# A spectral mixing layer and an ELU feed-forward on one core: tokens ordered by quarters, x read in strided chunks, the first batch's start rearranged

## The chip, the cores and the metric

The kernel runs on one core of a Trainium2 chip. The metric is the device time in microseconds; of several runs the median counts. Engines are named as in the profile: PE (TensorE, with PEld for its weight loads), DVE (VectorE), ACT (ScalarE), POOL (GpSimd) and SP (SyncE, here only an issuer of DMAs).

## The reference

For each of 8 batches of 3008 tokens by 256 channels: a real Fourier transform along the tokens, a complex linear layer with a soft threshold, the inverse transform; then a feed-forward with ELU over all tokens.

```python
X = np.fft.rfft(x, axis=1)
Yr = Xr @ w_r - Xi @ w_i + b_r
Yi = Xr @ w_i + Xi @ w_r + b_i
Yr = np.sign(Yr) * np.maximum(np.abs(Yr) - lam, 0.0)      # Yi likewise
y = np.fft.irfft(Yr + 1j * Yi, n=3008, axis=1)
h = y @ w_in                                              # 256 -> 2048
g = np.where(h > 0.0, h, np.exp(np.minimum(h, 0.0)) - 1.0)
out = g @ w_out                                           # 2048 -> 256
```

## The kernel before

The Fourier transform of length 3008 is split into 47 x 64, so a token has two indices; in the code a token is `r * 32 + n`, with `r` of 94 and `n`, the second index, of 32. Everything is written as matrix products with tables made on the chip from sines.

A batch goes through these units, each a few matmuls on PE into PSUM, followed by one copy out:

- **A** (8 units, L111): the first short transform. `load_x` (L93) reads x in four chunks of 8 neighbouring `n`, on POOL's queue, as two DMAs of 80 and 14 partitions; a partition gets 8 neighbouring rows, 8 KB in one piece. Two units work on a chunk; the result goes to DRAM (`DA`).
- **Z** (`load_Z`, L138): three pieces read back from `DA`, turned so that the other index lies on the partitions. A piece is four DMAs.
- **X** (6 units, L148): the second short transform, two units (`dt` 0 and 1) a piece, copied to `XT`.
- **M** (12 groups, L167 to L208): the complex linear layer, bias and soft threshold, giving `Y`. DVE adds the bias (`yb`); then POOL clips and subtracts, or, for some groups of batch 0, ACT clips and DVE finishes (`let_go`, one group later).
- **B** (6 units, L210): the first half of the inverse; to DRAM (`DB`), and read back as four tiles `Bs` (L240), one for each quarter of `n`.
- **Y** (8 units, L249): the second half. Units `2w` and `2w + 1` take the `Bs` of quarter `w` and write `yT`, the transposed input of the feed-forward. Before the change the tokens of `yT` lie in their natural order, so that each unit writes 8 of every 32 tokens.

The **feed-forward** runs over all 8 batches as one stream of steps. A batch has 48: six blocks of tokens (five of 512, one of 448), and in each eight pairs of feature tiles. `front(i)` (L521) makes `hps` with four matmuls and starts ACT's Exp (`Et`); `elu` (L539) makes `gT` with two DVE instructions; `back(i - 2)` (L547) adds to the block's output in PSUM with eight matmuls, and at a block's end ACT copies it to `osb` and SP issues its DMA, one for all whole tiles of 128 tokens and one for the rest. Since a block's tokens lie across all of `n`, its first `front` needs all eight Y units of its batch.

The order on every engine is the order in which the program is written (`tc.manual_schedule()`); an engine works its queue strictly in turn. `plan(b)` (L591) places units into the steps of batch `b`: list `f1` between `front` and `elu`, list `f2` behind `back`. In batch `b` run X, M, B and Y of batch `b + 1` and A of batch `b + 2`; batch 0 also carries A of batch 1, and the last batch carries nothing. In batches 1 to 6 the units X to A lie in steps 2 to 33, Y in steps 40 to 47. The units of the loop share one PSUM tile (`psF`, L507).

**Batch 0** goes through the units ahead of the loop ("alone"), with PSUM pools of its own (`pre2`, `pre1`, `pre0`, L72 to L74). Two things stand in the order there: DVE computes the sine arguments for the table M2 (`wrap`, L315) in three groups, ACT turns them into sines behind that group's copies of A (L363 to L382), and `idle_pe` (L266) issues matmuls whose result nobody reads, which keep PE at work while it would wait. Behind them come the load of the feed-forward's weights, X, M and B of batch 0 (L468 to L492), the reading of `Bs`, 28 idle matmuls, and eight Y units. `gate` (L452) makes POOL wait for a tile before it issues the loads behind it.

## Time and profile before

| | us |
|---|---|
| median of three runs | 1008.99 (1007.75 to 1010.56) |
| the profiled execution | 1007.92 |
| its span, first to last instruction | 1005.8 |
| first `gT` of the loop starts | 87.13 |
| batches 1 to 5, each | about 115.7 |

A profile page shows the busy time of each engine, the span in slices, the DMA queues, the chain of work that ended last, the costliest groups of instructions and the DMAs. A row of the timeline gives the start, the busy time, the engine, the line, the operation, the tiles with their shape, and in brackets the idle time before it and what ended that. A row of the windows gives the stretch, its length, each engine's busy time with its count of instructions, the clock granted to PE (1.00 is full), the share of the DMA engines and the bytes they moved.

### The profile page before, as it was taken

The numbers are of one execution on the slowest core, as the hardware profiler recorded it, in microseconds if no ns is written. First come the engines' busy times: TensorE is split into PE (matmuls) and PEld (weight loads), VectorE is DVE, ScalarE is ACT, GpSimd is POOL, SyncE is SP. The second block draws the span as 40 slices with busy tenths as digits, with TensorE's granted clock in tenths as the row PEclk, the third lists the DMA queues.
The fourth block names the chain that finished last, engine by engine and source line by source line (L and its number), as shares of the span: only waits on it lengthen the run. The fifth ranks groups of instructions, "written<-read, shape, count | busy, mean of one in ns | idle before, by whom it ended". The sixth has DMA issues, their size and how long they took to land.

```text
span 1005.8 us, 16444 instructions
## 1 busy us (share of the span) xinstructions
PE 939.9 (93%) x6469; PEld 660.6 (66%) x6469; DVE 831.7 (83%) x935; ACT 625.0 (62%) x722; POOL 249.5 (25%) x262
## 2 busy tenths in 40 slices
PE   3777899999999999999999999999999999999997
PEld 1335666676667666776667766676667766677775
DVE  8346778789888998889988898889988888888886
ACT  4235666865676657675586566675676656575554
POOL 4232155015400453005500354005410144000000
PEclk9888999999999999999999999999999999999999
DMA  9939451924292244713373053812446011400011
GB/s 192 244 90 219 119 134 44 236 64 104 73 251 53 68 107 117 186 41 83 94 197 107 21 138 84 236 40 52 116 123 159 19 43 56 113 30 33 22 42 40
DMA packets 91714, 105.41 MB, mean 105 GB/s; under 512 B 5682, under 2 KB 81460, under 8 KB 88628
## 3 DMA queue, kind: packets, MB, share of 16 engines
q1 hardware_dynamic: 84916, 76.04, 27.3%
q0 software_dynamic: 6176, 26.74, 12.8%
q10 hardware_dynamic: 544, 1.57, 0.7%
q8 instruction: 51, 0.84, 0.4%
q14 instruction: 27, 0.22, 0.1%
HBM read 54.53 MB, written 49.81 MB: 104 GB/s over the span
## 4 chain that ended last, share of the span: by engine, by line
PE 69%; DVE 13%; ACT 10%; DMA 5%; issue 2%; POOL 0%; ACTq 0%; DVEq 0%; SPq 0%; POOLq 0%
PE hps L531 28%; PE ps_o L564 24%; DVE gT L542 8%; PE mps L172 8%; ACT Et L536 6%; DVE Et L540 4%; PE aps L120 3%; PE bps L220 3%; DMA DA<-A 2%; PE xps L156 2%; PE yps L257 2%; ACT XT L109 1%; DMA Bs<-DB 1%; DMA xt<-in_x_dram 1%; ACT yT L109 1%
## 5 line engine op out<-in xcount | busy, mean ns | idle before, releaser
L536 ACT ACTIVATE Et<-hps 128x1024 f32<-128x1024 f32 (+1 forms) x384 | 388.6, 1012 | 316.7 <-PE hps L531 314.9
L542 DVE SCALAR_TENSOR_TENSOR gT<-hps,Et 128x1024 fp32r<-128x1024 f32 (+1 forms) x384 | 461.7, 1202 | 34.9 <-DVE Et L540 0.9
L564 PE MATMUL ps_o<-w_out_r,gT 128*128 128x256 f32 (+1 forms) x3072 | 473.2, 296 | 2.1 <-ACT osb L576 1.3
L564 PEld LDWEIGHTS ps_o<-w_out_r,gT 128*128 128x128 f32 (+1 forms) x3072 | 403.9, 187 | 47.4 <-issue 8.9
L531 PE MATMUL hps<-yT,w_in_s 128*128 128x512 bf16 (+1 forms) x1536 | 392.8, 377 | 21.5 <-DVE gT L542 19.4
L540 DVE TENSOR_SCALAR Et<-Et 128x1024 f32<-128x1024 f32 (+1 forms) x384 | 279.9, 729 | 79.3 <-ACT Et L536 78.2
L531 PEld LDWEIGHTS <-w_in_s 128*128 128x128 bf16 x1536 | 127.5, 97 | 138.2 <-issue 30.8
L187 POOL TENSOR_SCALAR clip<-yb 128x512 f32<-128x512 f32 x84 | 77.0, 917 | 510.1 <-DVE yb L179 509.5
L188 POOL TENSOR_TENSOR Y<-yb,clip 128x512 bf16<-128x512 f32 x84 | 108.1, 1286 | 7.0
L179 DVE TENSOR_TENSOR yb<-mps,bias_bc 128x512 f32<-128x512 f32 x96 | 66.2, 691 | 28.9 <-PE mps L172 22.0
L172 PEld LDWEIGHTS <-XT 128*128 128x128 bf16 x384 | 37.6, 99 | 53.1 <-ACT XT L109 5.8
L109 ACT CAST A<-aps 96x1024 bf16<-96x1024 f32 x63 | 62.9, 1003 | 13.1 <-PE aps L120 8.4
L120 PE MATMUL aps<-xt,M 94*96 94x512 f32 x128 | 50.8, 487 | 16.9 <-DMA xt<-in_x_dram 10.9
L172 PE MATMUL mps<-wcat_r,XT 128*128 128x512 bf16 x192 | 59.0, 387 | 5.3 <-ACT XT L109 5.0
L172 PE MATMUL mps<-wcat_s,XT 128*128 128x512 bf16 x192 | 58.2, 385 | 0.0
L109 ACT CAST yT<-yps 128x752 bf16<-128x752 f32 x60 | 47.1, 785 | 12.9 <-PE yps L257 12.9
L576 ACT COPY osb<-ps_o 128x512 f32<-128x512 f32 x96 | 50.4, 586 | 3.7 <-PE ps_o L564 3.7
L97 POOL DMA_DIRECT2D xt<-in_x_dram x64 | 44.0, 690 | 32.1 <-PE aps L120 31.8
L109 ACT CAST XT<-xps 128x1024 bf16<-128x1024 f32 x47 | 47.1, 1006 | 7.6 <-PE xps L156 7.6
L109 ACT CAST Bz<-bps 128x1024 bf16<-128x1024 f32 x47 | 47.8, 1019 | 2.3 <-PE bps L220 2.3
L120 PEld LDWEIGHTS aps<-xt,M 94*96 94x96 f32 x128 | 20.1, 176 | 33.4 <-ACT A L109 19.0
L257 PEld LDWEIGHTS <-Bs 96*128 96x128 bf16 x512 | 28.5, 100 | 16.4 <-DMA Bs<-DB 4.5
(76 smaller groups left out, 234.1 us busy)
## 6 DMA issues: line engine op xcount, KB each, us to landing
xt<-in_x_dram POOLq DMA_DIRECT2D x32, 640.0 KB, 6.1
out_dram<-osb SPq DMA_DIRECT2D x40, 512.0 KB, 3.4
Z<-DA SPq DMA_DIRECT2D x90, 128.0 KB, 3.4
Bs<-DB SPq DMA_DIRECT2D x60, 192.0 KB, 4.6
DA<-A SPq DMA_DIRECT2D x28, 384.0 KB, 4.4
DB<-Bz SPq DMA_DIRECT2D x21, 512.0 KB, 3.4
xt<-in_x_dram POOLq DMA_DIRECT2D x32, 112.0 KB, 5.7
out_dram<-osb SPq DMA_DIRECT2D x8, 384.0 KB, 2.6
```

The lines of the kernel that those rows point to most:

```text
L109: nc.scalar.copy(dst, src)
L120: nc.tensor.matmul(ps[0 : 4 * K1, j, :], lhsT=M1[:], rhs=xt[:, 4 * uu + 2 * j : 4 * uu + 2 * j + 2, :], start=True, stop=True,)
L172: nc.tensor.matmul(ps, lhsT=XT[:, dt, c, o : o + P], rhs=wm[:, dt, :], start=(m == 0 and dt == 0), stop=(m == 1 and dt == 1),)
L179: nc.vector.tensor_tensor(yb[:], ps, bias_bc[:], ALU.add)
L187: nc.gpsimd.tensor_scalar(clip[:], yb[:], LAM, -LAM, ALU.min, ALU.max)
L188: nc.gpsimd.tensor_tensor(Y_of[b, q][:, i, :], yb[:], clip[:], ALU.subtract)
L531: nc.tensor.matmul(hps[:, s, 0:nb], lhsT=w_in_s[:, dt, ft * P : ft * P + P], rhs=yT[:, dt, bs : bs + nb], start=(dt == 0), stop=(dt == 1),)
L536: nc.scalar.activation(Et[:, :, 0:nb], hps[:, :, 0:nb], AF.Exp)
L540: nc.vector.tensor_scalar(Et[:, :, 0:nb], Et[:, :, 0:nb], 1.0, -1.0, ALU.min, ALU.add)
L542: nc.vector.scalar_tensor_tensor(gT[:, :, 0:nb], hps[:, :, 0:nb], 0.0, Et[:, :, 0:nb], ALU.max, ALU.add)
L564: nc.tensor.matmul(po[q][0 : t1 - t0, i_ % 2, :], lhsT=gT[:, s, t0:t1], rhs=w_out_r[:, ft, :], start=(ft == 0 and i_ % 2 == 0), stop=(ft = ...
L576: nc.scalar.copy(osb[:, i_ : i_ + k, :], po[i_ // 2][:, 0:k, :])
```

## The change

The order of tokens in `yT` becomes (quarter `w` of `n`, `r`, place `j` in the quarter), so a unit of Y writes 752 neighbouring tokens and a block needs only the quarters it lies in. The output's DMAs put the rows back in order: one for each 128 tokens, and two where a tile lies across two quarters. Ahead of the loop stand only Y units 0 and 1 of batch 0; units 2 to 7 of every batch now run inside that batch's own steps, units 0 and 1 of the next one behind `back` in steps 46 and 47. Chunk `ci` of x holds the `n` of the form `4 m + ci`, so a partition gets 8 rows of 1 KB instead of one piece of 8 KB; A's writes follow that. In batch 0, A's tiles lie in the four buffers of `Bs`, X units 0 to 3 stand ahead of all M, units 4 and 5 between the first M groups, and `XT` has three buffers. The idle matmuls read a constant tile, have a PSUM bank for themselves, and stand at more places: 20 at the start, 5, 5 and 3 behind units of A, 16 (14 before) ahead of X. The bias copy moves from ACT to DVE. The load of batch 1's x waits for the last `Bs` instead of the first `yT`.

```diff
-        xv = x[b].rearrange("(r n) d -> r n d", n=NH)
+        xv = x[b].rearrange("(r m c) d -> c r m d", c=4, m=8)
-            nc.gpsimd.dma_start(xt[r0:r1], xv[r0:r1, ci * 8 : ci * 8 + 8, :].bitcast(F32R))
+            nc.gpsimd.dma_start(xt[r0:r1], xv[ci, r0:r1].bitcast(F32R))
...
-            A_of[b, ci] = wk2.tile([4 * K1, 8, D], BF16, name="A", tag="A")
+            if alone:
+                A_of[b, ci] = wk4.tile([4 * K1, 8, D], BF16, name="A", tag="Bs")
+            else:
+                A_of[b, ci] = wk2.tile([4 * K1, 8, D], BF16, name="A", tag="A")
...
+        dav = DA_of[b].rearrange("(m c) r d -> c r m d", c=4)
...
+            nc.sync.dma_start(dav[ci, :, 4 * uu : 4 * uu + 4, :], A[:, 4 * uu : 4 * uu + 4, :])
...
+            nc.sync.dma_start(dav[ci], A[:])
...
-                engs[h].dma_start(Z[q : q + NH], DA_of[b][:, r : r + 8, :])
+                engs[c].dma_start(Z[q : q + NH], DA_of[b][:, r : r + 8, :])
...
-            XT_of[b, g] = wk2.tile([P, 2, 2, 8 * N2], BF16, name="XT", tag="XT")
+            XT_of[b, g] = wk3.tile([P, 2, 2, 8 * N2], BF16, name="XT", tag="XT")
...
-            yT[:, dt, :].rearrange("p (r n) -> p r n", n=NH)[:, :, 8 * w : 8 * w + 8],
-            psv[:, :, 0 : 2 * N1].rearrange("p n r -> p r n"), on_dve,
+            yT[:, dt, w * WT : w * WT + WT].rearrange("p (r j) -> p r j", j=8),
+            psv[:, :, 0 : 2 * N1].rearrange("p j r -> p r j"), on_dve,
...
+    busy = constp.tile([P, 512], BF16, name="busy")
+    nc.vector.memset(busy[:], 1.0)
+    ips = pre0.tile([P, 512], F32, name="ips", tag="pre0")
...
+            nc.tensor.matmul(ips[:], lhsT=busy[:, 0:P], rhs=busy[:], start=True, stop=True)
...
+    idle_pe(20)
...
-            if g == 2:
+            if g < 2:
+                idle_pe(5)
+            else:
+                idle_pe(3)
                 unit_A(0, 6, alone=True)
                 unit_A(0, 7, alone=True, on_dve=True)
...
-        m4ps = pre0.tile([P, 512], F32, name="m4ps", tag="pre0")
+        m4ps = pre1.tile([P, 512], F32, name="m4ps", tag="mps1")
...
-        bb = pre0.tile([P, 2 * D], F32, name="bb", tag="pre0")
+        bb = pre1.tile([P, 2 * D], F32, name="bb", tag="mps1")
-        nc.scalar.copy(bias_bc[:], bb[:])
-        idle_pe(14)
+        nc.vector.tensor_copy(bias_bc[:], bb[:])
+        idle_pe(16)
...
     fX(1, True)
+    fX(2)
+    fX(3, True)
     first_M(0, 0, True)
+    fX(4)
     first_M(0, 1, False)
+    fX(5)
     first_M(1, 0, True)
     first_M(1, 1, False)
-    fX(2)
-    fX(3)
     first_M(2, 0, True)
+    fB(0)
...
-    for u in range(8):
+    for u in range(2):
         unit_Y(0, u, alone=True, on_dve=bool(u % 2))
-    gate(yT_of[0][:, 0, 0:1])
+    gate(Bs_of[0, 3][:, 0, 0:1])
...
+        ov = out[b * S : b * S + S, :].rearrange("(r w j) e -> w r j e", w=4, j=8)
+        for q in range((nsub + 1) // 2):
...
+            for i_ in range(2 * q, 2 * q + k):
+                t, end = bs + i_ * P, min(bs + i_ * P + P, bs + nb)
+                while t < end:
+                    w, r0 = t // WT, t % WT // 8
+                    t1 = min(end, (w + 1) * WT)
+                    p0, n8 = t - bs - i_ * P, (t1 - t) // 8
+                    nc.sync.dma_start(
+                        ov[w, r0 : r0 + n8], osb[p0 : p0 + 8 * n8, i_, :]
+                    )
+                    t = t1
...
         if b == 0:
+            for u in range(2, 8):
+                f1[u - 1].append(put("Y", 0, u))
             for u in range(8):
-                f1[2 + u].append(put("A", 1, u))
+                f1[7 + u].append(put("A", 1, u))
-            lead, pairs = 13, [
+            lead, seq = 18, [
...
-            lead, pairs = 2, [[u] for u in (
+            lead, seq = 0, [
+                ("y", 2), ("y", 3), ("X", 0), ("X", 1), ("M", 0, 0), ("M", 0, 1), ("X", 2),
+                ("M", 1, 0), ("M", 1, 1), ("X", 3), ("B", 0), ("y", 4), ("M", 2, 0), ("M", 2, 1),
+                ("y", 5), ("X", 4), ("B", 1), ("M", 3, 0), ("M", 3, 1), ("X", 5), ("B", 2),
+                ("y", 6), ("M", 4, 0), ("M", 4, 1), ("B", 3), ("y", 7), ("M", 5, 0), ("M", 5, 1),
+                ("A", 0), ("B", 4), ("A", 1), ("B", 5), ("A", 2), ("A", 3), ("A", 4), ("A", 5),
+                ("A", 6), ("A", 7),
...
+        if n1 < B:
+            for u in range(2):
+                f2[46 + u].append(put("Y", n1, u))
```

In the lists `("y", u)` is unit `u` of Y of the batch whose steps run, the other entries are of the next batch (A of the one after it). `WT` is 752.

More of the change, by code (lines that the diff above doesn't have):

```diff
@@ L80 @@
     LAG = 2
+    WT = 2 * N1 * 8
     x_of = {}
@@ L261, in unit_Y @@
         evac(
-            yT[:, dt, :].rearrange("p (r n) -> p r n", n=NH)[:, :, 8 * w : 8 * w + 8],
-            psv[:, :, 0 : 2 * N1].rearrange("p n r -> p r n"), on_dve,
-        )
+            yT[:, dt, w * WT : w * WT + WT].rearrange("p (r j) -> p r j", j=8),
+            psv[:, :, 0 : 2 * N1].rearrange("p j r -> p r j"), on_dve,
+        )
+    busy = constp.tile([P, 512], BF16, name="busy")
+    nc.vector.memset(busy[:], 1.0)
+    ips = pre0.tile([P, 512], F32, name="ips", tag="pre0")
     def idle_pe(n):
-        ps = pre0.tile([P, 512], F32, name="idle", tag="pre0")
         for _ in range(n):
-            nc.tensor.matmul(
-                ps[:], lhsT=M2[:, 0, 0:2, :].rearrange("p a b -> p (a b)"),
-                rhs=M2[:, 0, 0:8, :].rearrange("p a b -> p (a b)"), start=True, stop=True,
-            )
+            nc.tensor.matmul(ips[:], lhsT=busy[:, 0:P], rhs=busy[:], start=True, stop=True)
+    idle_pe(20)
     with tc.tile_pool(name="stagep", bufs=1) as stagep:
@@ L571, in back @@
         osb = late2.tile([P, 4, E], F32, name="osb", tag="osb")
-        nfull, rem = nb // P, nb % P
-        row0 = b * S + bs
-        for i_ in range(0, nfull, 2):
-            k = min(2, nfull - i_)
-            nc.scalar.copy(osb[:, i_ : i_ + k, :], po[i_ // 2][:, 0:k, :])
-        nc.sync.dma_start(
-            out[row0 : row0 + nfull * P, :].rearrange("(i p) e -> p i e", p=P),
-            osb[:, 0:nfull, :],
-        )
-        if rem:
-            nc.scalar.copy(osb[0:rem, nfull, :], po[nfull // 2][0:rem, nfull % 2, :])
-            nc.sync.dma_start(
-                out[row0 + nfull * P : row0 + nb, :], osb[0:rem, nfull, :]
-            )
+        ov = out[b * S : b * S + S, :].rearrange("(r w j) e -> w r j e", w=4, j=8)
+        for q in range((nsub + 1) // 2):
+            k = min(2, nsub - 2 * q)
+            if nb >= (2 * q + k) * P:
+                nc.scalar.copy(osb[:, 2 * q : 2 * q + k, :], po[q][:, 0:k, :])
+            else:
+                for e in range(k):
+                    rows = min(P, nb - (2 * q + e) * P)
+                    nc.scalar.copy(osb[0:rows, 2 * q + e, :], po[q][0:rows, e, :])
+            for i_ in range(2 * q, 2 * q + k):
[8 more added lines that the diff above has]
+                    t = t1
         del po_of[b, blk]
@@ L594, in plan @@
         f2 = [[] for _ in range(PER)]
-        if b + 1 >= B:
-            return f1, f2
         n1, n2 = b + 1, b + 2
-        def at(t, *us, r=f1):
-            for u in us:
-                r[t].append(put(u[0], n2 if u[0] == "A" else n1, *u[1:]))
         if b == 0:
+            for u in range(2, 8):
+                f1[u - 1].append(put("Y", 0, u))
             for u in range(8):
-                f1[2 + u].append(put("A", 1, u))
-            f1[9] += [(load_Z, (1, g)) for g in range(3)]
-            lead, pairs = 13, [
[6 rows of a table removed]
+                f1[7 + u].append(put("A", 1, u))
+            f1[14] += [(load_Z, (1, g)) for g in range(3)]
+            lead, seq = 18, [
[5 rows of a table added]
             ]
-            xs = (12, 15, 18, 21)
+            xs = (16, 19, 22, 25)
         else:
-            lead, pairs = 2, [[u] for u in (
[5 rows of a table removed]
-            )]
-            xs = (3, 7, 11, 15)
-        for t, us in enumerate(pairs, lead):
-            us = [u for u in us if n2 < B or u[0] != "A"]
-            at(t, *us[:1])
-            at(t, *us[1:], r=f2)
-            if ("A", 3 if b == 0 else 4) in pairs[t - lead]:
+            lead, seq = 0, [
[6 rows of a table added]
+            ]
+            xs = (3, 7, 11, 15)
+        for t, u in enumerate(seq, lead):
+            if u[0] == "y":
+                f1[t].append(put("Y", b, u[1]))
+            elif u[0] == "A":
+                if n2 < B:
+                    f1[t].append(put("A", n2, u[1]))
+            elif n1 < B:
+                if u[0] == "X" and len(u) == 3:
+                    f1[t].append(put("X", n1, u[1]))
+                    f2[t].append(put("X", n1, u[2]))
+                else:
+                    f1[t].append(put(u[0], n1, *u[1:]))
+            if u == ("A", 3) and n1 < B:
                 f2[t] += [(load_Bs, (n1, w)) for w in range(4)]
@@ L634, in plan @@
                 f1[xs[ci]].append((load_x, (n2, ci)))
-        for u in range(8):
-            at(40 + u, ("Y", u), r=f2 if f1[40 + u] else f1)
+        if n1 < B:
+            for u in range(2):
+                f2[46 + u].append(put("Y", n1, u))
         return f1, f2
```

16 lines of the change are left out of this document (3 added, 13 removed), and 16 rows, old and new, of tables (f2, xs).

## The prediction

> **What bounds the kernel now.** I read the page's first part, then the busy time by stage (the cuts are the moments at which one kind of work hands over to the next), then the chain of waits.
>
> ```profile
> PE 939.9 (93%) x6469; PEld 660.6 (66%) x6469; DVE 831.7 (83%) x935; ACT 625.0 (62%) x722; POOL 249.5 (25%) x262
> ```
>
> ```profile
> core 0: us, PE busy (x) PEld busy (x) DVE busy (x) ACT busy (x) POOL busy (x), PEclk, DMA share, GB/s
> 0.00:27.55 27.55, 10.01 (x34) 5.62 (x35) 22.05 (x53) 13.03 (x17) 11.58 (x22) 1.00 0.88 188
> 27.55:37.48 9.93, 6.93 (x27) 3.05 (x24) 1.38 (x2) 0.58 (x1) 0.89 (x2) 0.83 0.89 235
> 37.48:68.81 31.33, 22.44 (x149) 10.28 (x148) 15.62 (x21) 13.60 (x16) 13.64 (x14) 0.86 0.61 147
> 68.81:83.02 14.21, 10.21 (x90) 6.00 (x89) 5.43 (x8) 3.14 (x4) 4.45 (x9) 0.86 0.91 207
> 83.02:87.13 4.11, 3.73 (x8) 1.09 (x8) 1.43 (x2) 1.17 (x2) 0.00 (x0) 0.50 1.13 223
> ...
> 210.86:326.54 115.68, 113.51 (x802) 80.77 (x801) 100.39 (x108) 77.14 (x90) 31.94 (x32) 1.00 0.43 109
> ```
>
> From 87 us on TensorE is busy 98% of a batch at full clock: the loop is bound by the work put into its steps. Before 87 us five stages run one after the other. Only in the first is an engine near full (VectorE, 22 of 27.55 us); the others have the clock at 0.5 to 0.86 and are held by waits. That is where the change works. The chain of waits names the holders:
>
> ```profile
> 23.98 1.22 DVE A L107
> ...
> 25.22 2.23 DMA DA<-A
> ...
> 27.98 3.96 DMA Z<-DA
> ...
> 32.30 0.59 ACT bias_bc L423
> ...
> 32.94 4.70 PE idle L270 x14
> ...
> 68.83 2.79 DMA DB<-Bz
> ...
> 73.01 8.28 DMA Bs<-DB
> ```
>
> All sums below are against this profiled execution (span 1005.8, 1007.92 with what lies around it); the median of the runs, 1008.99, lies 1.07 above it.
>
> **Stage 1, x and A (0 to 27.55).** Two things change: x comes in 1 KB pieces instead of 8 KB, and A gets four buffers.
>
> ```profile
> 1.39 2.30 POOL L97 DMA_DIRECT2D xt<-in_x_dram  x4 [0.18 <-issue]
> ...
> 20.41 0.69 DVE L318 TENSOR_TENSOR v<-r,v 128x512 f32<-128x512 f32 x1
> 20.74 1.92 ACT L109 CAST A<-aps 96x1024 bf16<-96x1024 f32 x2 [3.55 <-DMA DA<-A]
> ```
>
> ```profile
> L450 POOL DMA_DIRECT2D w_out_r<-in_moe_w_out_dram x2 | 1.9, 952 | 0.3 <-issue 0.3
> ```
>
> ```profile
> 41.00:46.00 5.00, 3.16 (x27) 1.81 (x25) 3.75 (x5) 1.53 (x3) 3.76 (x4) 1.00 1.84 354
> ```
>
> Speed of the load: w_out, in 1 KB pieces, flows at 354 GB/s (41 to 46 us); x of batch 1, in 8 KB pieces, at 223 (83 to 87 us). So small pieces cost nothing here, and x is likely to land earlier. That gains nothing by itself, since ScalarE's copies of A stand behind the sines, and these behind VectorE's sine arguments. Issue: a w_out DMA of 1,024 pieces held POOL for 952 ns; four x DMAs of 80 and 14 pieces held it 2.30 us, 575 each. Their new counts are 640 and 112, so by a line between the two rows (0.4 ns a piece) the four take 2.8 us (+0.5); all at 952 would be +1.5. kv is queued behind them on POOL, and VectorE's long run of sine arguments behind kv: +0.5 on that run, which ended at 21.10 and will end at 21.6. The wait of 3.55 us (ScalarE for an A buffer) goes; what is late next is that VectorE run, behind which the last A's copy stands: 1.22 + 2.23 for its DMA, so Z can be issued at about 25.2 instead of 27.55: **-2.35** (bounds +1, if all of kv's and more delay comes, to -3).
>
> The 33 new idle matmuls lie in TensorE's 17 free microseconds of this stage; even at half clock the first 20 end (20 x 0.43) by the time A can start. Their memset runs while VectorE still waits for POOL's first iota. Z's four DMAs a piece are split between SP and ScalarE's queue by c instead of h, two on each as before: nothing.
>
> **Stage 2, Z to the first X (27.55 to 37.48).** Z's first piece has landed by 31.94, yet X starts at 37.48 (the cut): ScalarE issues Z's DMAs, then the bias copy (32.30), and the 14 idle matmuls wait for that bank, 4.70 us. After: the copy is on VectorE and the idle matmuls have a bank of their own, so they follow `bb`.
>
> ```profile
> 25.57 0.15 PEld L404 LDWEIGHTS m4ps<-ident,M1p 94*96 94x96 f32 x1 [2.46 <-issue]
> ...
> 28.45 1.49 PE L422 MATMUL bb<-brow,ones 1*128 1x512 f32 x2
> ```
>
> `bb` ends 4.37 us after the M4 transpose, which follows the last A's copy by 0.37 (25.20 to 25.57): now 22.85 + 0.37 + 4.37 = 27.6. Sixteen matmuls then take 3.45 us at full clock (0.215 each, rows of stage 3) or 5.1 with eight at half clock: X at 31.05 to 32.7. Z lands at 25.2 + 4.4 = 29.6, before that. I take 32.0, in between: the stage is 6.8 instead of 9.93, **-3.1** (bounds -2 to -5). M3's third bank now waits for M4's copy and `bb` for M3's first copy; both copies are done while the transposes run.
>
> The row of 14 idle matmuls in 4.70 us is a start at half clock. [...]
>
> **Stage 3, X, M and B (37.48 to 68.81).**
>
> ```profile
> 46.87 0.61 PE L172 MATMUL mps<-wcat_r,XT 128*128 128x512 bf16 x1 [2.71 <-ACT XT L109]
> 47.78 0.61 PE L172 MATMUL mps<-wcat_r,XT 128*128 128x512 bf16 x1 [0.30 <-ACT XT L109]
> 48.18 1.06 PE L172 MATMUL mps<-wcat_s,XT 128*128 128x512 bf16 x2
> 49.03 1.06 PE L172 MATMUL mps<-wcat_r,XT 128*128 128x512 bf16 x2
> ...
> 53.33 0.59 PE L172 MATMUL mps<-wcat_r,XT 128*128 128x512 bf16 x2
> 53.76 0.59 PE L172 MATMUL mps<-wcat_s,XT 128*128 128x512 bf16 x2
> ...
> 57.19 0.61 PE L156 MATMUL xps<-M,Z 128*128 128x128 bf16 x8 [1.74 <-ACT Bz L109]
> ...
> 59.02 0.39 PE L172 MATMUL mps<-wcat_r,XT 128*128 128x512 bf16 x1 [0.53 <-ACT XT L109]
> ```
>
> Twice TensorE waits for X evacuations that stand on ScalarE behind clips: 2.71 + 0.30 + 1.74 + 0.53 = 5.3 us. After the first wait matmuls run at half clock (two in 0.85 us from 48.18 to 49.03, two in 0.43 from 53.33 to 53.76), from 47.78 to about 52.7: half of 4.9, 2.45 us. With X 0 to 3 ahead of all M and X 4 and 5 between the first M's, with a third XT buffer, the evacuations are done before their M's come: both terms go. 31.33 - 7.7 = 23.6: **-7.7**. Low end -9.5 (TensorE's 22.44 less 2.45 is 20, and copies must follow), high end -3.7 (half comes back as a wait for VectorE, whose 15.62 us get one more X copy and the bias).
>
> **Stage 4, B to the loop (68.81 to 83.02).** DB and Bs are the same: the last B's DMA, Bs issue, first Bs landed.
>
> ```profile
> 76.36 0.79 ACT L109 CAST yT<-yps 128x752 bf16<-128x752 f32 x1 [8.89 <-PE yps L257]
> 76.70 0.94 DVE L107 CAST yT<-yps 128x752 bf16<-128x752 f32 x1 [5.49 <-PE yps L257]
> ```
>
> The rows are the first two Y's. Two Y units, not eight, stand before the first hps: it starts at 77.15 on this clock, not 83.02: 8.3 instead of 14.21, **-5.9** (bounds -5 to -6.5). The other Bs land within 5 us, before their units come. x of batch 1 now waits for the last Bs, not for yT; behind that gate on POOL are only those loads, and the A units that need them start at step 7, over 15 us later.
>
> **Stage 5, to the first gT (83.02 to 87.13).** The clock is 0.50 here after the Y waits. With the idle matmuls just ahead, hps runs at full clock: eight matmuls, 8 x 0.215 = 1.7 us less, of which the first four lie ahead of the first gT: **-0.9** (0 to -1.7).
>
> **The loop (87.13 to the end).** Four windows cut at gT starts (columns: VectorE's gT time and count, clock, DMA share, GB/s):
>
> ```profile
> 515.90:525.10 9.20, 4.90 (x4) 1.00 0.97 228
> 952.20:973.20 21.00, 12.24 (x10) 1.00 0.11 38
> 540.20:555.10 14.90, 7.64 (x7) 1.00 0.11 37
> 985.70:999.10 13.40, 7.64 (x7) 1.00 0.12 41
> ```
>
> Four steps with an A unit take 2.30 us each, ten plain ones of the last batch 2.10; in the short last block a step with Y takes 2.13, a plain one 1.91. A unit costs 0.20 or 0.22 in either place (I price a Y in a full block like an A), so moving Y among the steps is worth nothing either way. Y's copy writes the same 752 elements, now side by side: the same price. New in the loop are the six Y's that left the prologue: the count in batches 0 to 6 stays, the last batch gets six: 6 x 0.2 = **+1.2** (0.6 to 3).
>
> ```profile
> 100.77 1.01 ACT L109 CAST A<-aps 96x1024 bf16<-96x1024 f32 x1 [1.12 <-DMA DA<-A]
> ```
>
> This wait in batch 0, A's DMA behind the x load, goes, since A comes five steps later, when x is in: **-1.1**. The last A of batch 2 now stands at step 46, four steps (9.2 us) before that batch's first X: Exp and copy 2.0, DMA 2.2 or more, issue 0.1 to 0.8, Z 4.0 (stage rows above) make 8.3 to 10: **+0.5** (0 to 2).
>
> ```profile
> 1002.47 0.47 SPq L583 DMA_DIRECT2D out_dram<-osb  x1
> ```
>
> Output leaves in 27 DMAs a batch instead of 7. At 0.4 to 0.5 us of issue that is 9 us more of SP in 116; queued behind them on SP are A's, Z's, B's and Bs' DMAs, none needed within the next steps but that Z, which is ahead of them. At the end two more issues stand on the path, part of it beside the copies: **+0.4**. Loop: **+1.0** (-3 to +5, as a shifted pattern of 0.5 us a batch would give).
>
> **Sum.** -2.35 - 3.1 - 7.7 - 5.9 - 0.9 + 1.0 = -18.95: span 986.9, execution 989.0, median 990.0, so **990**.
>
> **The rivals.**
> - *Half of stage 3 comes back.* VectorE gets X's second copy twice and the bias, and shares the chain M, clip, Y with POOL. For it: 15.62 and 13.64 us of work with strict order. Against it: 23.6 leaves both about a third idle. +3.7: 994.
> - *The loop pays.* Two Y's end a batch and two begin the next, just where ScalarE copies osb, and units share one PSUM buffer. If each of seven seams costs 0.8: +5.6, 996. Against: A units in successive steps hold 2.30.
> - *POOL starves.* POOL's lists of pieces for x and VectorE's f32 runs get in each other's way: kv 1.5 us late and VectorE's run stretched by 2 more: +3, 993. [...]
> - *More goes.* Stage 3 at its floor and the pattern of steps better by 0.4 a batch: 985.
> - *Slower: false waits on yT.* Now Y writes one quarter of the yT tile that the hps of the same batch read. If the wait is on the whole tile, each of 48 Y's in the loop stops the next hps until its copy is done:
>
> ```profile
> 94.97 1.00 ACT L109 CAST A<-aps 96x1024 bf16<-96x1024 f32 x1
> ...
> 95.26 1.04 PE L531 MATMUL hps<-yT,w_in_s 128*128 128x512 bf16 x4
> ```
>
> a unit's copy ends 0.71 after the next hps has begun; with Y's 0.79 us for 1.0 that is a stall of 0.5 to 0.7, 24 to 34 us in all: 1014 to 1024. It decides from 0.39 us a unit. Against it: the M matmul at 46.87 began on the first half of XT and the one at 47.78 on the second, so parts of a tile are told apart.
>
> **How the numbers follow.** Forecast 0.55; half of stage 3 back 0.15; loop pays 0.11; POOL starves 0.08; more goes 0.07; slower 0.04. The likeliest gives 990. The range for 8 in 10 takes all but the slower case and the ends of the others: 983 to 998 (the stages' bounds alone, -9.7 to -25.7 beside -19.95, will hardly all fall on one side). About 0.3% (3 us) is what a measurement of this kernel can tell from no change: faster 0.95, same 0.01, slower 0.04.
>
> **What would show it.** Right: Z issued near 25, the first X near 32, the last B copy near 56, hps near 64 with the clock near 1.0 through these stages, batches of 115 to 116, the last one 1 us longer. Wrong: VectorE's run past 23; X waiting for idle matmuls still; TensorE waiting over 1 us for X copies in stage 3; TensorE waiting for yT copies in the loop, or for Z at step 2 of batch 1. What would upset the whole is a steady batch 2 us longer: eight times that outweighs any single stage.

## The result

| | before | after |
|---|---|---|
| median of the runs, us | 1008.59 (1007.75 to 1010.56, 4 runs) | 986.03 (985.30 to 987.90, 4 runs) |
| profiled execution, us | 1007.92 | 985.79 |
| its span, us | 1005.8 | 983.9 |
| first `gT` starts, us | 87.13 | 66.98 |

The ratio of after to before is 0.9776 (95% interval 0.9756 to 0.9797). The forecast was 990.0 with a range of 983 to 998.

The busy time by stage of the kernel after, cut at the same events as that of before in the prediction, with batches 1 and 2 of the loop behind it (columns: stretch, its length, each engine's busy time and count, granted clock, DMA share, GB/s):

```profile
0.00:25.68 25.68, 16.55 (x69) 8.10 (x70) 22.45 (x55) 12.92 (x17) 12.86 (x22) 0.86 1.34 202
25.68:33.71 8.03, 7.70 (x26) 3.01 (x24) 2.05 (x3) 0.00 (x0) 0.00 (x0) 0.60 0.87 230
33.71:56.01 22.30, 18.39 (x149) 9.52 (x151) 16.79 (x22) 12.76 (x15) 14.55 (x15) 1.00 0.93 232
56.01:63.79 7.78, 5.72 (x40) 2.77 (x38) 2.90 (x5) 0.79 (x1) 0.00 (x0) 1.00 0.73 181
63.79:66.98 3.19, 2.33 (x15) 1.17 (x16) 1.13 (x3) 1.86 (x3) 0.00 (x0) 1.00 0.69 162
191.36:307.28 115.92, 112.49 (x789) 80.72 (x801) 98.59 (x109) 77.52 (x89) 33.67 (x32) 1.00 0.55 122
307.28:421.89 114.61, 112.56 (x789) 80.82 (x801) 98.51 (x109) 77.39 (x89) 33.70 (x32) 1.00 0.50 110
```

Beside the rows of before this gives, in microseconds:

| stage | before | after | gain | predicted |
|---|---|---|---|---|
| 1, x and A | 27.55 | 25.68 | 1.87 | 2.35 |
| 2, Z to the first X | 9.93 | 8.03 | 1.90 | 3.1 |
| 3, X, M and B | 31.33 | 22.30 | 9.03 | 7.7 |
| 4, B to the loop | 14.21 | 7.78 | 6.43 | 5.9 |
| 5, to the first `gT` | 4.11 | 3.19 | 0.92 | 0.9 |
| loop, to the end | 918.7 | 916.9 | 1.7 | -1.0 |

Of the 21.9 us that the span lost, 20.2 lie ahead of the loop, where 19.95 were forecast; that the sum fits so closely is luck, since stages 1 and 2 gave 1.7 less than forecast and stages 3 and 4 gave 1.9 more. The loop was to lose 1.0 and gained 1.7. Stage 3 is now at full clock (1.00 instead of 0.86). Stage 2 is the worst of what is left: TensorE is busy 7.70 of its 8.03 us, but at a clock of 0.60, and most of it is work that nobody reads. The chain of waits of the kernel after (start, us, engine and what it did) shows that, and the new bound of stage 1:

```profile
7.93 11.83 DMA xt<-in_x_dram
19.89 2.01 PE aps L125 x4
21.92 1.22 DVE A L108
...
23.91 2.56 PE m3ps L420 x24
26.47 2.00 PE bb L426 x2
...
28.80 5.07 PE ips L273 x15
33.87 0.91 PE xps L156 x16
```

Before, the chain went through `DA<-A` into stage 1's end; now it is the last x that A waits for, and behind A the M3 transposes, the bias product and the idle matmuls stand one after the other.

### The profile page after: what moved, and what is told of

Its sections match the earlier page's. It is cut to its first block, busy times and chain, and to the rows that moved or that the text cites. A ratio compares the mean times of both kernels' runs of the same rounds, so it can differ in the third digit from the quotient of the medians.

```text
span 983.9 us, 16644 instructions
## 1 busy us (share of the span) xinstructions
PE 934.0 (95%) x6400; PEld 661.4 (67%) x6504; DVE 822.6 (84%) x935; ACT 627.1 (64%) x723; POOL 261.9 (27%) x262
## 4 chain that ended last, share of the span: by engine, by line
PE 71%; ACT 11%; DVE 10%; issue 3%; DMA 3%; POOL 1%; another core or an unknown queue 0%; SPq 0%; DVEq 0%; ACTq 0%; POOLq 0%
PE hps L535 26%; PE ps_o L568 26%; PE mps L172 8%; DVE gT L546 6%; ACT Et L540 5%; DVE Et L544 3%; PE bps L220 3%; PE yps L257 2%; PE xps L156 2%; PE aps L125 2%; ACT A L110 2%; DMA xt<-in_x_dram 1%; ACT osb L580 1%; ACT XT L110 1%; DMA DA<-A 1%
## 5 line engine op out<-in xcount | busy, mean ns | idle before, releaser
L535 PE MATMUL hps<-yT,w_in_s 128*128 128x512 bf16 (+1 forms) x1436 | 385.3, 377 | 21.8 <-DVE gT L546 10.4
L544 DVE TENSOR_SCALAR Et<-Et 128x1024 f32<-128x1024 f32 (+1 forms) x384 | 269.1, 701 | 82.2 <-ACT Et L540 77.3
L187 POOL TENSOR_SCALAR clip<-yb 128x512 f32<-128x512 f32 x84 | 79.4, 945 | 494.1 <-DVE yb L179 493.8
L188 POOL TENSOR_TENSOR Y<-yb,clip 128x512 bf16<-128x512 f32 x84 | 111.1, 1322 | 7.0
L98 POOL DMA_DIRECT2D xt<-in_x_dram x64 | 50.7, 795 | 33.3 <-PE aps L125 32.8
L110 ACT CAST yT<-yps 128x752 bf16<-128x752 f32 x63 | 49.2, 780 | 13.9 <-PE yps L257 13.9
L172 PE MATMUL mps<-wcat_r,XT 128*128 128x512 bf16 x191 | 56.9, 379 | 0.6 <-ACT XT L110 0.5
L125 PE MATMUL aps<-xt,M 94*96 94x512 f32 x128 | 48.5, 466 | 7.7 <-DMA xt<-in_x_dram 4.6
L580 ACT COPY osb<-ps_o 128x512 f32<-128x512 f32 x88 | 48.1, 600 | 5.5 <-PE ps_o L568 5.5
L156 PEld LDWEIGHTS <-Z 128*128 128x128 bf16 x384 | 25.1, 98 | 17.2 <-issue 8.2
```

The lines of the kernel that those rows point to most:

```text
L110: nc.scalar.copy(dst, src)
L125: nc.tensor.matmul(ps[0 : 4 * K1, j, :], lhsT=M1[:], rhs=xt[:, 4 * uu + 2 * j : 4 * uu + 2 * j + 2, :], start=True, stop=True,)
L172: nc.tensor.matmul(ps, lhsT=XT[:, dt, c, o : o + P], rhs=wm[:, dt, :], start=(m == 0 and dt == 0), stop=(m == 1 and dt == 1),)
L187: nc.gpsimd.tensor_scalar(clip[:], yb[:], LAM, -LAM, ALU.min, ALU.max)
L188: nc.gpsimd.tensor_tensor(Y_of[b, q][:, i, :], yb[:], clip[:], ALU.subtract)
L535: nc.tensor.matmul(hps[:, s, 0:nb], lhsT=w_in_s[:, dt, ft * P : ft * P + P], rhs=yT[:, dt, bs : bs + nb], start=(dt == 0), stop=(dt == 1),)
```

## The experiments

Each kernel is the kernel after with one edit, unless said otherwise. Where one run is given, a difference under 2 us says little (the four runs of after spread over 2.6), so what follows is read from the stage in the trace. Stage 2 and batch 0 moreover vary with the same code. For stage 2 the clock rows further down show it. Batch 0 of the loop took 124.0 to 124.4 us where a stretch of half clock falls into its first steps (the kernel after, experiments 8 and 10) and 122.4 to 122.7 where none does (experiments 2, 3, 6 and 9, with the same batch 0). The stretch in the kernel after, in which step 2 took 3.71 us instead of the 2.23 of experiment 9:

```profile
69.71:73.13 3.42, 3.42 (x17) 2.23 (x17) 2.34 (x3) 1.41 (x3) 3.42 (x5) 0.50 1.98 209
```

### 1. Eight neighbouring rows of x in one piece, as before

```diff
-        xv = x[b].rearrange("(r m c) d -> c r m d", c=4, m=8)
+        xv = x[b].rearrange("(r n) d -> r n d", n=NH)
-            nc.gpsimd.dma_start(xt[r0:r1], xv[ci, r0:r1].bitcast(F32R))
+            nc.gpsimd.dma_start(xt[r0:r1], xv[r0:r1, ci * 8 : ci * 8 + 8, :].bitcast(F32R))
-        dav = DA_of[b].rearrange("(m c) r d -> c r m d", c=4)
+        dav = DA_of[b].rearrange("(c m) r d -> c r m d", c=4)
```

> The changed kernel with x read as before, 8 neighbouring rows in one piece of 8 KB (A's writes to DRAM follow). Theory: the size of the pieces is worth nothing; x flows at about 210 GB/s in either form, the last x lands near 19.8 us, Z is issued within 0.5 us of 25.7, and the span stays at 983.9 within 1.5 us. Rival 1, small pieces flow faster: x lands 3 us or more later, Z issued near 29, span near 987. Rival 2, POOL's longer lists cost: kv comes 0.5 us sooner, Z is issued near 25.2, VectorE's run is shorter, span near 983.

984.44 us in one run (before 1008.97 beside it). Z is issued at 24.71 instead of 25.68. The queue's rows for the first 26 us (queue, packets, MB, packet time as a share of 16 engines) are, for the kernel after:

```profile
q0 software_dynamic: 3200, 3.08, 102.3%
```

and with pieces of 8 KB:

```profile
q0 software_dynamic: 512, 3.08, 54.8%
```

The times of the packets for the same 3.08 MB sum to nearly twice as much in short pieces: about 133 ns for each of 3,200 packets (1.023 x 26 us x 16 / 3,200). In the chain of the 8 KB kernel stage 1 is no longer held by x: it is VectorE's run of sine arguments up to the last A copy, of which the last two pieces are:

```profile
20.40 0.69 DVE v L319
21.09 1.13 DVE A L108
```

So the short pieces are what A waits for in the kernel after. Its last four A matmuls run at half clock besides (2.01 us at a clock of 0.50; 1.14 in experiment 4, where x is late all the same). At Z the short pieces cost about 1 us instead of nothing: all runs with them and four buffers issue Z at 25.7 to 26.7, the three with 8 KB pieces at 24.7, 25.2 and 25.9 (the last two from experiments 11 and 12, which change more). None of that reached the first X in this run, which started at 33.60 instead of 33.71 behind a stage 2 of 8.90 us; the shorter span (982.6 instead of 983.9) comes from batch 0, 2.0 us shorter without a half-clock stretch.

### 2. Two buffers for A, as before

```diff
-            if alone:
-                A_of[b, ci] = wk4.tile([4 * K1, 8, D], BF16, name="A", tag="Bs")
-            else:
-                A_of[b, ci] = wk2.tile([4 * K1, 8, D], BF16, name="A", tag="A")
+            A_of[b, ci] = wk2.tile([4 * K1, 8, D], BF16, name="A", tag="A")
```

> The changed kernel with A of batch 0 in two buffers as before. Theory: ScalarE again waits for an A buffer until the first A writes have landed, behind the x load: its third pair of copies starts near 20.5 to 21 instead of 17.4, Z is issued 1.5 to 2 us later (27.3 to 27.7), everything behind it shifts by as much, span near 985.6. Rival: the x load alone sets this stage (the last x lands near 19.8 in any case), so the copies catch up and Z is issued within 0.5 us of 25.7, span 984.

986.85 us in one run. Z is issued at 27.94, 2.3 us later, and the first `gT` starts 2.8 later (69.76). The timeline of ScalarE shows the old wait again:

```profile
21.16 1.92 ACT L110 CAST A<-aps 96x1024 bf16<-96x1024 f32 x2 [3.30 <-DMA DA<-A]
```

and the chain of this kernel says what it waits for, a DMA of 8.53 us beside the x load, at a DMA share of 1.28 in this stage (the last A's DMA of before took 2.23):

```profile
12.53 8.53 DMA DA<-A
```

The four buffers are worth 1.3 to 2.3 us (against Z issued at 26.7 or 25.7), which is about the whole gain of stage 1 (1.87).

### 3. The old order of X, M and B in batch 0

```diff
     fX(0)
     fX(1, True)
-    fX(2)
-    fX(3, True)
     first_M(0, 0, True)
-    fX(4)
     first_M(0, 1, False)
-    fX(5)
     first_M(1, 0, True)
     first_M(1, 1, False)
+    fX(2)
+    fX(3)
...
```

> The changed kernel with the order of X, M and B of batch 0 as before (X 2 and 3 behind the fourth M, X 4 and 5 behind B 1, all copied by ScalarE). Theory: the stage from the first X to the last B copy goes from 22.3 back to 30 to 31.5 us, with two waits of TensorE of 1.5 us or more for X copies and matmuls at half clock behind the first, span near 992. Rival: the third XT buffer and the warm clock give most of the gain, so the stage is 24 to 27 us, span 986 to 988.

992.59 us in one run. Stage 3 takes 31.01 us again (windows, then rows of TensorE's timeline):

```profile
33.51:64.52 31.01, 21.08 (x147) 10.08 (x148) 15.28 (x21) 13.60 (x16) 14.51 (x15) 0.91 0.66 173
```

```profile
43.44 0.39 PE L172 MATMUL mps<-wcat_r,XT 128*128 128x512 bf16 x1 [3.24 <-ACT XT L110]
44.58 0.59 PE L172 MATMUL mps<-wcat_s,XT 128*128 128x512 bf16 x2 [0.75 <-ACT XT L110]
...
52.83 0.61 PE L156 MATMUL xps<-M,Z 128*128 128x128 bf16 x8 [1.74 <-ACT Bz L110]
```

These are the waits of before (2.71, 0.30 and 1.74 there), though the third `XT` buffer and the idle matmuls are in. So 8.7 of the 9.0 us are the order of X, M and B, with the engine of one copy that goes with it (X 3's is back on ScalarE).

### 4. Eight Y units ahead of the loop

```diff
-    for u in range(2):
+    for u in range(8):
         unit_Y(0, u, alone=True, on_dve=bool(u % 2))
...
         if b == 0:
-            for u in range(2, 8):
-                f1[u - 1].append(put("Y", 0, u))
```

> The changed kernel with all eight Y units of batch 0 ahead of the loop and none of them in its steps (order of tokens as changed). Theory: from the last B copy to the first hps it takes 12 to 14 us instead of 7.8, and hps starts at half clock; batch 0's steps get 1.2 us back; span near 988 to 990. Rival: the time is given back by the loop, which then has six units less: span 984 to 985.

990.11 us in one run. Stages 2, 4 and 5 of this kernel:

```profile
26.65:30.76 4.11, 3.36 (x15) 1.36 (x15) 0.53 (x1) 0.00 (x0) 0.00 (x0) 1.00 0.74 209
...
55.35:68.97 13.62, 9.80 (x90) 5.92 (x89) 6.18 (x9) 3.15 (x4) 2.23 (x4) 0.88 0.62 147
68.97:72.80 3.83, 3.35 (x7) 1.17 (x8) 0.77 (x1) 1.24 (x2) 3.22 (x6) 0.50 1.89 217
```

Stage 4 grows by 5.84 and stage 5 by 0.64, and its clock falls to 0.50 as before the change. That is the size the prediction gave to stage 4. The first row shows something else: stage 2 is the same code as in the kernel after and takes 4.11 instead of 8.03 us, at a clock of 1.00 instead of 0.60.

### 5. Four empty steps in the old order of the loop

The kernel before, with steps 11, 14, 21 and 25 of batches 1 to 6 left free, about where the kernel after has its Y units, and the later units moved back:

```diff
-            lead, pairs = 2, [[u] for u in (
+            lead, pairs = 2, [[u] if u else [] for u in (
...
-                ("X", 3), ("B", 0), ("M", 2, 0), ("M", 2, 1), ("X", 4), ...
+                ("X", 3), ("B", 0), None, ("M", 2, 0), ("M", 2, 1), None, ("X", 4), ...
-                ("X", 5), ("B", 2), ("M", 4, 0), ("M", 4, 1), ("B", 3), ("M", 5, 0), ...
+                ("X", 5), ("B", 2), None, ("M", 4, 0), ("M", 4, 1), ("B", 3), None, ("M", 5, 0), ...
```

> The kernel before, with nothing changed but four empty steps (11, 14, 21 and 25) put into the list of units of batches 1 and up, where the changed kernel has Y units. Theory: the changed kernel's steady batches are 1 us shorter because these gaps move VectorE's Et instruction away from POOL's subtraction, which it waits for; so here the three Et of 1.69 us in each batch go to 0.9 or less, the three steps of 3.28 go, and a batch takes 113.5 to 115 instead of 115.7, span 996 to 1002. Rival: it comes from where the Y units stand (the short last block or the full ones), or from the order of tokens: batches stay at 115.7 within 0.3, span 1004.5 to 1007.

1000.79 us in one run (before 1007.61 beside it); batch 2 by its window:

```profile
326.52:440.57 114.05, 112.89 (x803) 80.61 (x802) 98.54 (x109) 77.25 (x90) 31.89 (x32) 1.00 0.43 110
```

The loop of before thus gets 1.6 us a batch out of where its units stand, with the same work. In the step times (from one `gT` start to the next) three steps of 3.28 us became one.

### 6. The last four Y's doubled up with other units

```diff
-                ("M", 1, 0), ("M", 1, 1), ("X", 3), ("B", 0), ("y", 4), ("M", 2, 0), ("M", 2, 1),
+                ("M", 1, 0), ("M", 1, 1), ("X", 3), ("B", 0), ("M", 2, 0), ("M", 2, 1),
...
+        if b:
+            for u, t in ((4, 9), (5, 13), (6, 17), (7, 29)):
+                f2[t].append(put("Y", b, u))
```

Likewise for `("y", 5)` to `("y", 7)`.

> The changed kernel with Y units 4 to 7 of batches 1 and up behind the eight back matmuls of steps that hold another unit (9, 13, 17, 29), so that X, M, B and A stand in the steps that they had before. Theory (the gaps): long Et instructions of over 1.2 us come back, two or three a batch, and a steady batch takes 115.2 to 116.5 instead of 114.6, span 988 to 996. Rival (the gaps don't matter): no Et over 1.0 us, a batch within 0.4 of 114.6, span 982 to 987.

1011.65 us in one run, slower than before; neither number was met. Batch 2, and the step with X 3 and Y 4 in batch 1:

```profile
310.30:429.65 119.35, 114.29 (x802) 81.44 (x801) 97.85 (x109) 77.54 (x90) 34.08 (x32) 1.00 0.49 105
```

```profile
211.54 0.61 PE L156 MATMUL xps<-M,Z 128*128 128x128 bf16 x8
...
213.72 0.49 PE L257 MATMUL yps<-M,Bs 96*128 96x94 bf16 x8 [0.56 <-ACT XT L110]
...
215.40 0.61 PE L220 MATMUL bps<-Y,M 64*128 64x256 bf16 x8 [0.32 <-ACT yT L110]
```

The cost is not VectorE's: the units of the loop share one PSUM tile, so the second unit of a step waits for the first one's copy, and the unit of the next step for the second's. Four doubled steps make a batch 4.7 us longer than in the kernel after (119.35 against 114.61), so a Y costs about 1.2 more as the second unit of a step than in a step of its own. This is why the kernel after must spend a step of its own on each Y. The long `Et`'s of the expectation didn't come back (none over 1 us in batches 1 to 4, one in batch 5). That the four empty steps help in the old order for the same reason is likely, but not shown.

### 7. The x loads of the loop issued behind the M pairs

What made the 3.28 us steps of before? In the timeline of batch 2, in the first of them (step 8), VectorE's first `elu` instruction takes 1.70 us instead of 0.68, while POOL subtracts:

```profile
345.26 1.53 POOL L97 DMA_DIRECT2D xt<-in_x_dram  x2
...
347.53 1.27 POOL L188 TENSOR_TENSOR Y<-yb,clip 128x512 bf16<-128x512 f32 x1
347.65 1.70 DVE L540 TENSOR_SCALAR Et<-Et 128x1024 f32<-128x1024 f32 x1 [0.25 <-ACT Et L536]
```

The issue of an x load (1.53 us on POOL) stands between the two groups of an M pair, so the second group's clip and subtraction come late and meet `Et`. The kernel before, with the loads moved:

```diff
-            xs = (3, 7, 11, 15)
+            xs = (3, 9, 13, 17)
```

> The kernel before, with the loads of the next x in the loop issued at steps 3, 9, 13 and 17 of a batch instead of 3, 7, 11 and 15, so that none stands between the two groups of an M pair on POOL; no empty step is added. Theory (what the empty steps gained is that VectorE's Et no longer meets POOL's subtraction, and it met it because an x issue of 1.5 us on POOL held the second group's clip and subtraction back by about 1 us): the 3.28 us steps and the Et's over 1.0 us go, batches 1 to 5 take 114.0 to 114.4 us instead of 115.67, span about 998, execution 999 to 1001. Rival (empty steps gain by giving the shared PSUM tile and the copies time): no step is added here, so batches stay at 115.6 to 115.7 and the time at 1008.

1005.0 us (1004.71 to 1006.45, 4 runs), ratio to before 0.9956 (0.9939 to 0.9974). Batch 2, and the same place in it:

```profile
327.96:442.90 114.94, 112.63 (x790) 80.51 (x802) 98.23 (x108) 77.16 (x89) 32.11 (x32) 1.00 0.42 109
```

```profile
348.20 1.29 POOL L188 TENSOR_TENSOR Y<-yb,clip 128x512 bf16<-128x512 f32 x1
349.16 0.88 DVE L540 TENSOR_SCALAR Et<-Et 128x1024 f32<-128x1024 f32 x1 [0.25 <-ACT Et L536]
```

No `Et` is over 0.9 us any more (three in each of batches 1 to 5 were). A batch gains 0.74 us, not the 1.3 to 1.7 expected: the collision is real, but it is less than half of what the empty steps gave. They removed two of the three collisions, some 0.5 us by this run; that leaves 1.1 for the units standing further apart, which fits experiment 6. That share was not isolated.

### 8. Y units 0 and 1 of the next batch in steps 44 and 45

The kernel after places them behind `back` in steps 46 and 47, and there TensorE waits at the start of the next batch:

```profile
419.18 0.81 PE L535 MATMUL hps<-yT,w_in_s 128*128 128x512 bf16 x2 [0.66 <-ACT yT L110]
```

```diff
-                f2[46 + u].append(put("Y", n1, u))
+                (f1[44 + u] if b else f2[46 + u]).append(put("Y", n1, u))
```

> The changed kernel with Y units 0 and 1 of the next batch in steps 44 and 45 (ahead of the back matmuls), not behind those of steps 46 and 47, in batches 1 to 6. Theory: the first hps of a batch waits for the copy of Y unit 1 (0.66 us at 419.2) and the steps around it for ScalarE; with two steps between, steps 47 to 1 take 0.7 to 1.2 us less in each of six batches, span 977 to 980. Rival: a unit costs what it costs wherever it stands, so steps 44 and 45 grow by what 47 loses, span 983 to 985.

981.93 us in one run; a batch takes 0.67 us less, just under the expected 0.7, and six seams 3.9:

```profile
306.70:420.64 113.94, 113.04 (x802) 80.75 (x801) 98.42 (x108) 77.20 (x89) 33.71 (x32) 1.00 0.51 110
```

The last step of a batch falls from 3.15 to 2.33 us. This is the rival "the loop pays at its seams" at nearly its forecast price (0.8).

The same trace shows what an earlier first X is worth. Its stage 2, with the code of the kernel after, took 4.26 us, so X began at 30.95 instead of 33.71; yet the first `gT` starts at 67.03 instead of 66.98. In its chain POOL waits for the last piece of Z before it issues `w_out`, and its clips for M stand behind that; then come the 28 idle matmuls ahead of Y, up to 59.0 us at half clock:

```profile
36.05 0.19 POOL gate L459
...
53.97 8.66 PE ips L273 x28
```

### 9. Eight idle matmuls ahead of X instead of 16

```diff
-        idle_pe(16)
+        idle_pe(8)
```

> The changed kernel with 8 instead of 16 idle matmuls ahead of the first X. Theory: X waits for the idle matmuls and not for Z; eight of them at half clock take 3.4 us and have the clock up at their end, so X starts at 32.0 to 32.3 instead of 33.7 at full clock, and the span falls by 1.4 to 1.7, to 982.3. Rival 1: Z has not landed, X starts at 33 or later, span 983 to 984. Rival 2: the clock is not yet up, X and the first M run at half clock and the gain is given back, span 983.5 to 985.

983.84 us in one run. Stage 2 takes 5.83 us, 2.2 less, at a clock of 0.52. Stage 1 was 1.0 longer in this run, so X begins at 32.52 instead of 33.71, just behind the expected 32.0 to 32.3, and the first `gT` starts at 66.13 instead of 66.98. But stage 2 took 4.1 to 8.1 us with 16 idle matmuls too (see the clock rows below), so one run doesn't show that the shorter row is the cause. The span is 1.9 us shorter: 0.85 ahead of the loop and 1.8 in batch 0, which has no half-clock stretch, less 0.6 in batch 1.

### 10. The bias product early

```diff
+            if g == 0:
+                bb = pre1.tile([P, 2 * D], F32, name="bb", tag="mps1")
+                nc.tensor.matmul(bb[:], lhsT=ones[:], rhs=brow[:], start=True, stop=True)
             if g < 2:
                 idle_pe(5)
...
-        bb = pre1.tile([P, 2 * D], F32, name="bb", tag="mps1")
-        nc.tensor.matmul(bb[:], lhsT=ones[:], rhs=brow[:], start=True, stop=True)
-        nc.vector.tensor_copy(bias_bc[:], bb[:])
         idle_pe(16)
```

The copy of the bias and the memset of `ones` go ahead with it.

> The kernel after, with the bias product bb behind the first two A units and its copy ahead of the copy of M4, so that neither lies between the M3 transposes and the 16 idle matmuls. Theory (stage 2 is now bb at 2.07 us and the idle matmuls, in a row behind the M3 transposes): the idle matmuls begin about 2 us earlier, X starts at 30.0 to 31.7, where Z's landing some 4.2 us after its issue is next, span 981.5 to 982.5. Rival (the phase of the clock's window sets the start of X, not bb): X stays within 0.5 of 33.7 and the span at 983.5 to 984.5.

984.52 us in one run. Stage 2:

```profile
26.66:32.14 5.48, 5.26 (x23) 2.48 (x22) 1.34 (x2) 0.00 (x0) 0.00 (x0) 0.68 0.82 234
```

The stage is 2.55 us shorter, as the first theory has it; but Z was issued 1.0 later in this run, so X starts at 32.14, just past the expected 31.7, and the span of 982.7 lies 0.2 above its interval. The chain of the kernel after has both the row of idle matmuls and the bias product on the path. How much taking either off is worth stays open: 2.2 and 2.55 us lie inside what stage 2 varies by with the same code, and the first `gT` came only 0.85 and 0.6 us earlier.

### 11 and 12. What was learned, together

Edits 1, 8 and 10 with 10 idle matmuls; and the same with the x loads behind the M pairs:

```diff
-            xs = (16, 19, 22, 25)
+            xs = (16, 20, 23, 26)
...
-            xs = (3, 7, 11, 15)
+            xs = (3, 9, 11, 15)
```

> The kernel after with four edits: x in 8 KB pieces as before the change, the bias product early, 10 idle matmuls ahead of X instead of 16, and Y units 0 and 1 of the next batch in steps 44 and 45 ahead of elu (from batch 1 on). If what the single edits showed adds up (stage 1 -1.0, stage 2 -2.5, seams -0.65 x 6 = -3.9), the span is 976.5 and the execution 978.4, between 976 and 981. If the phase of the clock's window decides the first 35 us, stages 1 and 2 give under 1 us together and the execution is 981 to 982.

> The combined kernel with the loads of the next x issued behind the second group of an M pair: steps 16, 20, 23, 26 instead of 16, 19, 22, 25 in batch 0, and 9 instead of 7 for the second load of the other batches. Theory (an x issue between two groups of a pair pushes POOL's subtraction onto VectorE's Et): the Et's over 1.0 us, three in batch 0 and one in each of batches 1 to 5, go; batch 0 gets 0.7 to 1.5 us shorter, batches 1 to 5 0.2 to 0.3 each, the time 976 to 977.5 beside 979. Rival (where the issue stands makes no difference here, the long Et being covered): 978.5 to 979.5 with the same batches.

The first took 978.99 us (977.60 to 980.17, 4 runs), ratio to before 0.9699 (0.9681 to 0.9717), inside the expected range. The parts came out otherwise, though, in its profiled execution (span 977.9, expected 976.5): the first `gT` starts 2.8 us earlier where 3.5 were expected of stages 1 and 2, and batches 1 to 7 are 2.8 shorter where 3.9 were expected of the seams, because long `Et`'s came back. The second took 978.24 (976.66 to 979.47, 5 runs), ratio 0.9690 (0.9675 to 0.9706). The two sets of runs overlap, so the time leaves open whether the second step helps; the trace shows what was expected in part. The long `Et`'s (3 in batch 0, 1 in each of batches 1 to 5) are gone, and batches 1 to 5 are 0.14 to 0.28 shorter; batch 0 is only 0.15 shorter. The windows of the last kernel, stage 2 and batches 1 and 2:

```profile
25.91:30.07 4.16, 3.66 (x18) 1.81 (x17) 1.38 (x2) 0.00 (x0) 0.00 (x0) 0.70 0.72 217
...
187.53:302.93 115.40, 112.36 (x789) 80.60 (x801) 98.45 (x108) 77.30 (x89) 31.81 (x32) 1.00 0.48 123
302.93:416.90 113.97, 112.47 (x789) 80.77 (x801) 98.42 (x108) 77.20 (x89) 31.83 (x32) 1.00 0.45 110
```

Why did the long `Et` come back in the first of these? Experiment 1 has it too, in the same places (three in batch 0, one in each of batches 1 to 5); the kernel after has none from batch 1 on, though its load at step 7 also stands between the groups of a pair. Its rows:

```profile
211.93 1.83 POOL L98 DMA_DIRECT2D xt<-in_x_dram  x2
...
214.33 0.69 DVE L544 TENSOR_SCALAR Et<-Et 128x1024 f32<-128x1024 f32 x1 [0.25 <-ACT Et L540]
214.50 1.66 POOL L188 TENSOR_TENSOR Y<-yb,clip 128x512 bf16<-128x512 f32 x1
```

and those of the 8 KB kernel of experiment 1:

```profile
209.53 1.53 POOL L98 DMA_DIRECT2D xt<-in_x_dram  x2
...
211.81 1.28 POOL L188 TENSOR_TENSOR Y<-yb,clip 128x512 bf16<-128x512 f32 x1
211.93 1.70 DVE L544 TENSOR_SCALAR Et<-Et 128x1024 f32<-128x1024 f32 x1 [0.25 <-ACT Et L540]
```

With 8 KB pieces the issue takes 1.53, the subtraction begins 0.12 ahead of `Et`, and `Et` waits. With 1 KB pieces the issue takes 1.83, the subtraction begins 0.17 behind `Et`, and the subtraction waits (1.66 instead of 1.28), which nobody notices. So the dearer issue of the short pieces happens to pay here, by a margin under 0.2 us; it fits batch 2, 114.61 us against 114.84 in experiment 1. (In experiments 2, 4 and 6 one of the batches 1 to 5 has an `Et` of 1.2 us as well, but in other steps, 19 and 24, with no x load between the two groups.)

## Why the prediction was right, and where it was not

The sign, the order of the stages and the 20 us ahead of the loop were right; the time came out 4.0 us under the forecast: 2.7 of it in the loop, 0.2 ahead of it, and most of the rest because the median of after lies 0.2 above its profiled execution where 1.1 was taken over from before.

**Stage 1** (2.35 forecast, 1.87 measured). The A buffers do what was said (experiment 2). "Small pieces cost nothing here, and x is likely to land earlier" failed: the rate of `w_out` didn't carry over to x. Its packets took 85 ns each (180.8% of 16 engines over 5 us for 1,694 packets, from 41 to 46 us in before), those of x 133. Which difference makes that is open: x lands on 80 and 14 partitions instead of 128, shares the engines with the weights and A's writes, and VectorE works beside it on f32, as the rival *POOL starves* had it; no run separates these. The chain names x as the new bound, and experiment 1 sets the price at about 1 us at Z. The issue of four x loads, forecast at 2.8 us, took 2.81.

**Stage 2** (3.1, 1.90). The bank and the copy no longer hold anything, as said. But one of the named signs of being wrong came: X still waits for the idle matmuls. The mis-sized term is the clock. `bb` took 2.07 us at a clock of 0.50, where the sum had the 1.49 of before (1.12 in experiment 4, whose stage 2 has a clock of 1.00), and the idle matmuls 5.07, at 0.67, the sum's late end. The granted clock of the kernel after, in three windows:

```profile
15.10:18.51 3.41, 1.88 (x8) 0.78 (x7) 3.31 (x8) 2.67 (x5) 0.00 (x0) 1.00 1.76 229
18.51:32.16 13.65, 10.27 (x39) 5.44 (x41) 7.71 (x19) 4.32 (x6) 0.00 (x0) 0.50 0.80 218
32.16:35.57 3.41, 2.61 (x24) 1.62 (x23) 0.77 (x1) 1.01 (x1) 1.21 (x3) 1.00 0.90 253
```

Half clock lasted 13.65 us, four times 3.41. In the 8 KB kernel it was 10.24 us from 22.94, three times 3.41; in before it came in stretches of 3.41 us (from 32.68), 6.83 (46.33) and 3.42 (66.81), with 10.24 and 13.65 at full clock between them; in experiment 4, with the same code here, the clock was full from 18.3 on, and X began at 30.76. So in these runs the clock changes at distances that are multiples of 3.41 us, at places that differ from run to run, and the same 16 idle matmuls run at full clock or at half: in the kernels whose first two stages are those of after, stage 2 took 4.1 to 8.1 us. The first X was forecast at 32.0, inside its spread of 30.8 to 33.8; the 33.7 of the profiled run lies at the late end. Little of that spread goes on: where X began at 30.8 and 31.0 (experiments 4 and 8), stage 3 took 24.6 and 24.3 us instead of 22.3 and its last B copy ended at 55.4 and 55.2, beside 56.0 in the kernel after. So stages 2 and 3 are not independent terms, as the sum had them: a late stage 2 makes stage 3 look shorter.

**Stage 3** (7.7, 9.03). Waits and half clock went, and the order of X, M and B is the cause (experiment 3). The size is near the far bound (9.5): of waits over half a microsecond the timeline of TensorE keeps three, 1.31 for VectorE's first X copy, 1.53 for POOL's and 0.54 for VectorE's last Y. The first of them is over the 1 us that the prediction named as a sign of being wrong.

**Stages 4 and 5** (5.9 and 0.9; 6.43 and 0.92). Right, by experiment 4.

**The loop** (1.0 lost, 1.7 gained). The step that failed is "moving Y among the steps is worth nothing either way". It priced every unit at 0.2 us from windows in which units stand alone in a step, and took the steady batch of before as fixed. The runs point to three terms in its place, for a batch of the steady loop: the x loads no longer hold up POOL's second group at steps 11 and 15, and lose the race at step 7 (-0.74 by experiment 7); the units stand further apart (about -1.1, the rest of experiment 5, argued and not isolated); Y 0 and 1 at the seam cost +0.67 (experiment 8). Together -1.2, and batch 2 went from 115.67 to 114.61, -1.06. The end terms came as forecast in kind: the last batch +0.9 (forecast 1.2), the wait for Z in batch 1 about +1.3 by the two windows of the first table (115.92 against 114.61; forecast 0.5; a named sign of being wrong), and the tail +1.1 (forecast 0.4), since four issues now stand on SP behind the last copies:

```profile
978.61 0.64 ACT L584 COPY osb<-ps_o 128x256 f32<-128x256 f32 x2
978.74 2.56 SPq L591 DMA_DIRECT2D out_dram<-osb  x4
```

The wait in batch 1 stands in step 2, where X begins (in experiment 9 the profile puts the same wait, 2.02 us there, down to Z's DMA):

```profile
195.36 0.61 PE L156 MATMUL xps<-M,Z 128*128 128x128 bf16 x8 [1.44 <-ACT Et L540]
```

One more term of the loop failed: the wait for A's DMA in batch 0 was to go (-1.1), and 0.85 us of it is still there, five steps later:

```profile
93.15 1.01 ACT L110 CAST A<-aps 96x1024 bf16<-96x1024 f32 x1 [0.85 <-DMA DA<-A]
```

Batch 0 took 0.65 us more than before (124.38 against 123.73), with about 1.5 from the half-clock stretch in it. Batch 0 and batch 1 cost 0.9 us together, batches 2 to 6 gained 4.6, and the last with the tail cost 2.0: the 1.7 in all.

**The rivals.** *Half of stage 3 comes back*: no. *The loop pays*: its mechanism is there at nearly its price, but covered by a larger gain. *POOL starves*: no; VectorE's run in stage 1 ended 0.3 later, not 2. Whether POOL's lists and VectorE's f32 runs have a part in the slower x loads, the runs leave open. *More goes*: this came closest, at 986 against 985, and by the two parts it named, stage 3 near its floor and the pattern of steps. *False waits on yT*: no. The waits of TensorE for `yT` in a batch sum to 0.7 us, once at the seam, and that is a true wait for the quarter it reads.
